# More filler matmuls in TensorE's planned idle time, in a recurrence and feed-forward kernel

## The chip, the core and the metric

The kernel runs on one NeuronCore of one Trainium2 chip, as one program. The metric is the device time of one execution in microseconds (us), lower is better. TensorE (PE in the profile) multiplies matrices into PSUM; a matmul appears there as a weight load (PEld) and a matmul. VectorE (DVE), ScalarE (ACT) and GpSimd (POOL) do the elementwise work, and SyncE (SP) issues transfers. Each engine runs its own instructions in the order in which they were emitted, and waits for others through semaphores. The profile also records which clock TensorE was granted, as a share of full speed.

## What is computed

Two parts stand in a row: a gated linear recurrence per head, and a mixing block with a feed-forward network. Inputs are float32: q, k, v, alpha of (4 batches, 8 heads, 768 steps, 48), and weights of 384 x 1536 and 1536 x 384.

```
# recurrence, per batch and head; state is 48 x 48
for t in range(768):
    state = alpha[t][:, None] * state + outer(k[t], v[t])
    y[t] = q[t] @ state
x = y, heads side by side                          # (4, 768, 384)
u = x + real(fft(fft(x, axis=1), axis=2))
un = (u - mean(u)) / sqrt(var(u) + 1e-6)           # over the 384 columns
out = u + relu(un @ w_ch1) @ w_ch2
```

## The kernel before

**Work.** Heads are handled in pairs, four pairs to a batch. For a pair, VectorE scans alpha into running products (`al`, `w`), TensorE transposes (`kt<-al`), forms products of keys and queries (`f<-w,al`), ScalarE copies them to `w`, GpSimd masks them, and TensorE multiplies them with values (`a<-vn,w`) and carries the state on (`a<-tt,w`). When a batch's four pairs are done, its y goes through the transforms as matmuls with constant matrices (`f<-cst,w`, then `a<-cst,x`), VectorE adds the results to y and normalises the rows (`qs<-y,mv,r`), TensorE transposes those (`f<-cst,qs`), and the feed-forward network follows: `f<-x,wt` makes 128 hidden rows, ScalarE and VectorE split them into two parts `h`, and `f<-wt,h` accumulates the output. Batch 0's attention and transform have no feed-forward work beside them; later batches' run beside the feed-forward network of the batch before.

**Order.** The functions of the kernel do not issue instructions. They record operations, and a planner (`Plan.emit`) then walks through them with a duration for each operation and a clock for each engine in planned microseconds, and writes one order for all engines. The order depends on the planner's durations, on keys that the code sets (`plan.key`) and on when buffers come free. The chip then runs that order with its own durations.

**Fillers.** When the planner puts an operation on TensorE at planned time t, later than its clock for TensorE, it writes small matmuls ahead of it, as many as fit when each is given `DUMMY` of planned time:

```
if op.engine == "PE" and self.idle and t < self.idle[2] and not self.open:
    for _ in range(int((t - max(clock["PE"], self.idle[1])) / DUMMY)):
        order.append(self.idle[0])
```

`self.idle[1]` is 1.0, `self.idle[2]` is `WARM`: no filler is planned at or after that time. `self.open` is true while the PSUM tile that fillers write to (`f2`, number 2) accumulates a feed-forward output. The fillers don't move the planner's clock, so no other operation is planned differently for them. A filler multiplies a tile of zeros by itself, 32 columns wide, into a corner of that tile that nothing reads (line 1144 of the profile, `f<-zero`):

```
plan.idle = (lambda: nc.tensor.matmul(warm[2][0:32, 480:512], zero.real(), zero.real(), start=True, stop=True), 1.0, WARM, ("f2", 2))
```

Being float32 with two passes, each leaves two records in the profile. On the chip a filler is an ordinary instruction in TensorE's row: what stands behind it starts after it. Where the tile was read by ScalarE just before, the first filler behind waits for that read. In the profile line 463 is the helper that records all other operations, and line 211 the one for relu on ScalarE.

Of the kernel before, what the change touches and what calls it, by code (L numbers as in the profile page):

```python
# [53 lines left out]
SPLIT = 388  # L54
KCK = -700.0
KF0 = -505.0
WARM = 120.0
DUMMY = 0.11
KTINY = 0.5 * 2.0**15 / (1.0 + 15.5 / 128.0)


# [113 lines left out]
class Plan:  # L175
# [176 lines left out]
    def emit(self):  # L352
# [35 lines left out]
        while placed < len(ops):  # L388
# [35 lines left out]
# [3 lines that stand above are left out]
# [54 lines left out]
def gla_mix_ffn(ctx: ExitStack, tc: tile.TileContext, alpha, kq, v, w1, w2, consts, rowtab, out):  # L481
# [660 lines left out]
    warm = plan.tags["f2"]["reals"]  # L1142
    if WARM:
        plan.idle = (lambda: nc.tensor.matmul(warm[2][0:32, 480:512], zero.real(), zero.real(), start=True, stop=True), 1.0, WARM, ("f2", 2))  # L1144
    with tc.manual_schedule():
# [147 lines left out]
```

## Time and profile before

| | |
|---|---|
| median of 3 runs | 567.91 us (567.4 to 568.93) |
| profiled execution | 566.41 us, its span 564.7 us |
| TensorE busy | 537.7 us, 95% of the span |
| VectorE, ScalarE, GpSimd busy | 406.4, 194.8, 57.5 us |
| mean granted TensorE clock | 0.94 |
| fillers | 924 records, 44.0 us of TensorE's busy time |

The span runs from the first to the last instruction; the execution's own time is 1.7 us longer. Times in the profile count from the span's start. A row in order of time gives start and length, the engine, the line, the operation with its output and inputs (buffer numbers left out), its shape, and in brackets how long the engine sat idle before it and who ended that. Matmuls overlap, so their spacing is shorter than the duration of one. TensorE's clock is 1.00 or 0.50 at any moment; a stretch's figure is a mean.

### The profile page before, as it was taken

The page shows a single profiled execution, that of the slowest core. Times are in us where ns is not written, and L with a number is a line of the kernel's source. Part 1 is how long each engine was busy: PE and PEld are TensorE (multiplying, and loading weights), DVE is VectorE, ACT ScalarE, POOL GpSimd, SP SyncE. Part 2 cuts the span into 40 slices and gives each one's busy share as a digit, 9 for nine tenths or more (in the row PEclk, how much of TensorE's full clock was granted, in tenths as well). Part 3 has the DMA queues.
Part 4 walks back from the last instruction along what each step waited for, and adds up shares of the span by engine and source line. Part 5 has one row for each costly group of instructions (what it writes and reads, how often), then busy time and mean ns, then how long its engine had stood idle before and what let it go on. Part 6 is the DMA issues. An engine that isn't in the chain of part 4 may idle for free.

```text
span 564.7 us, 10382 instructions
## 1 busy us (share of the span) xinstructions
PE 537.7 (95%) x4144; PEld 520.9 (92%) x4144; DVE 406.4 (72%) x1078; ACT 194.8 (34%) x428; POOL 57.5 (10%) x80
## 2 busy tenths in 40 slices
PE   7799989789999999969999999999999999999995
PEld 6689979678999999959999999999999999999995
DVE  7746996999599968799998859999977672312111
ACT  3262523343463433123555232354451221211110
POOL 0221230010100112000112110021222000000000
PEclk9657987898799999979999999999999999999998
DMA  8996480010320025010342510112003000101001
GB/s 217 258 375 151 165 281 22 2 46 29 100 67 0 2 76 165 28 43 1 96 125 79 168 43 0 50 43 71 21 2 126 2 0 2 43 0 37 7 0 46
DMA packets 16549, 42.22 MB, mean 75 GB/s; under 512 B 1904, under 2 KB 7088, under 8 KB 16496
## 3 DMA queue, kind: packets, MB, share of 16 engines
q1 hardware_dynamic: 15440, 39.08, 22.7%
q0 software_dynamic: 768, 2.36, 1.5%
q8 instruction: 34, 0.56, 0.4%
q14 instruction: 19, 0.16, 0.1%
q10 hardware_dynamic: 288, 0.07, 0.1%
HBM read 34.42 MB, written 7.08 MB: 73 GB/s over the span
## 4 chain that ended last, share of the span: by engine, by line
PE 86%; DVE 6%; DMA 3%; ACT 1%; issue 1%; SPq 1%; POOL 0%; ACTq 0%
PE f L463 58%; PE a L463 24%; PE f L1144 4%; DMA al<-in_alpha_dram 3%; DVE y L463 2%; DVE w L463 1%; DVE st L463 1%; SPq L463 1%; DVE x L463 1%; DVE al L463 0%; ACT c L463 0%; DVE h L463 0%; ACT wt L463 0%; ACT x L463 0%; ACT w L463 0%
## 5 line engine op out<-in xcount | busy, mean ns | idle before, releaser
L463 PE MATMUL f<-x,wt 128*128 128x384 f32 x864 | 180.5, 347 | 0.1
L463 PE MATMUL f<-wt,h 128*128 128x384 f32 x864 | 179.2, 343 | 0.1
L463 PEld LDWEIGHTS f<-x,wt 128*128 128x128 f32 x864 | 154.0, 192 | 0.9 <-ACT x L463 0.5
L463 PEld LDWEIGHTS f<-wt,h 128*128 128x128 f32 x864 | 151.3, 190 | 1.2 <-issue 0.5
L463 DVE SCALAR_TENSOR_TENSOR h<-f,h 128x384 fp32r<-128x384 f32 x96 | 53.2, 555 | 82.2 <-ACT h L211 80.9
L211 ACT ACTIVATE h<-f 128x384 fp32r<-128x384 f32 x96 | 47.1, 491 | 183.6 <-PE f L463 171.4
L463 POOL TENSOR_SCALAR_AFFINE_SELECT w<-w 128x512 f32<-128x512 f32 (+1 forms) x64 | 43.2, 696 | 340.4 <-ACT w L463 335.2
L463 PE MATMUL a<-vn,w 128*128 128x64 f32 x312 | 50.2, 290 | 0.0
L1144 PEld LDWEIGHTS f<-zero 128*32 128x32 f32 x924 | 39.3, 128 | 10.4 <-ACT w L463 4.1
L1144 PE MATMUL f<-zero 128*32 128x32 f32 x924 | 44.0, 213 | 5.1 <-ACT w L463 3.7
L463 PEld LDWEIGHTS a<-vn,w 128*128 128x128 f32 x312 | 47.5, 214 | 0.5
L463 PE MATMUL a<-cst,w 96*128 96x96 f32 (+10 forms) x267 | 34.5, 271 | 4.2 <-DVE r L463 4.2
L463 PEld LDWEIGHTS a<-cst,w 128*96 128x96 f32 (+7 forms) x267 | 32.9, 169 | 5.4 <-issue 4.5
L463 ACT COPY w<-a 128x512 f32<-128x512 f32 (+6 forms) x58 | 25.7, 482 | 34.0 <-PE a L463 31.6
L463 DVE TENSOR_TENSOR y<-y,a 128x191 f32<-128x191 f32 (+2 forms) x96 | 27.8, 344 | 12.0 <-PE a L463 12.0
L463 PE MATMUL a<-qs,qs 112*128 112x256 f32 x162 | 30.0, 290 | 0.0
L463 PE MATMUL a<-tt,w 112*128 112x96 f32 x134 | 29.6, 305 | 0.0
L463 DVE TENSOR_TENSOR sd<-y,y 128x288 f32<-128x288 f32 x32 | 13.3, 454 | 22.1 <-ACT y L463 22.1
L463 DVE TENSOR_TENSOR_SCAN w<-al,d 112x768 f32<-112x768 f32 (+1 forms) x17 | 28.8, 1694 | 0.1
L463 DVE TENSOR_TENSOR_SCAN al<-al,d 112x768 f32<-112x768 f32 (+1 forms) x17 | 28.2, 1657 | 0.0
L463 DVE TENSOR_TENSOR y<-y,f 128x384 f32<-128x384 f32 (+2 forms) x44 | 21.1, 514 | 7.9 <-PE f L463 7.6
L463 PEld LDWEIGHTS a<-qs,qs 112*128 112x128 f32 x162 | 24.9, 189 | 0.0
(123 smaller groups left out, 626.1 us busy)
## 6 DMA issues: line engine op xcount, KB each, us to landing
kq<-in_kq_dram SPq DMA_DIRECT2D x13, 672.0 KB, 5.9
wt<-in_w_dram SPq DMA_DIRECT2D x8, 768.0 KB, 10.4
al<-in_alpha_dram SPq DMA_DIRECT2D x15, 336.0 KB, 5.4
out_dram<-y SPq DMA_DIRECT2D x24, 192.0 KB, 1.9
vn<-in_v_dram SPq DMA_DIRECT2D x14, 296.0 KB, 2.9
wt<-in_w_dram SPq DMA_DIRECT2D x8, 384.0 KB, 9.1
scr<-y SPq DMA_DIRECT2D x4, 576.0 KB, 4.1
wt<-in_kq_dram SPq DMA_DIRECT2D x2, 672.0 KB, 14.4
```

The costliest lines, as they stand in the source:

```text
L211: return lambda out, x: e.activation(out, x, AF.Relu)
L463: op.ins = op.fns[op.engine](*[real(a) for a in op.args], **{k: real(x) for k, x in op.kwargs.items()})
L1144: plan.idle = (lambda: nc.tensor.matmul(warm[2][0:32, 480:512], zero.real(), zero.real(), start=True, stop=True), 1.0, WARM, ("f2", 2))
```

## The change

```
-WARM = 120.0
-DUMMY = 0.11
+WARM = 150.0
+DUMMY = 0.04
```

The planner fits one filler into each 0.04 of planned idle time instead of 0.11, and may do so up to planned time 150 instead of 120. In the order that comes out, TensorE has 1304 fillers in place of 462, in the same 39 places; the last place is the same. All other instructions of TensorE stand as before, and so do those of the four other engines.

TensorE at the start of the program, with the change marked (`f_2_55_120<-zero` are fillers, `cst,al` transposes of keys, `vn,kt` the state's products, `w,al` keys by queries):

```order
 L1289 UNCONDITIONAL_BRANCH
-L1144 MATMUL f_2_55_120<-zero 32x32 x52
+L1144 MATMUL f_2_55_120<-zero 32x32 x145
 L463 MATMUL a_48_113<-cst,al_40_105 128x112 x3
-L1144 MATMUL f_2_55_120<-zero 32x32 x7
+L1144 MATMUL f_2_55_120<-zero 32x32 x21
 L463 MATMUL f_0_53_118<-vn_46_111,kt_9_74 112x96 x3
-L1144 MATMUL f_2_55_120<-zero 32x32 x13
+L1144 MATMUL f_2_55_120<-zero 32x32 x36
 L463 MATMUL f_0_51_116<-w_1_2_67,al_40_105 128x128
```

Nothing moved; the three blocks of fillers grew.

TensorE before, between the last attention product of batch 0 (`tt,w`) and its first transform matmuls (`cst,w`):

```order
L463 MATMUL f_1_123_753<-tt_135,w_1_95_539 128x2x48
L1144 MATMUL f_2_110_666<-zero 32x32 x81
L463 MATMUL f_0_134_938<-cst,w_6_7_72 97x65
L1144 MATMUL f_2_110_666<-zero 32x32
L463 MATMUL f_1_135_942<-cst,w_6_7_72 96x65
L1144 MATMUL f_2_110_666<-zero 32x32
L463 MATMUL a_136_946<-cst,w_6_7_72 95x64
L1144 MATMUL f_2_110_666<-zero 32x32 x10
```

The same place now (the last numbers in the names count tiles and differ for that reason alone):

```order
L463 MATMUL f_1_123_1062<-tt_135,w_1_95_781 128x2x48
L1144 MATMUL f_2_110_975<-zero 32x32 x224
L463 MATMUL f_0_134_1444<-cst,w_6_7_72 97x65
L1144 MATMUL f_2_110_975<-zero 32x32 x3
L463 MATMUL f_1_135_1450<-cst,w_6_7_72 96x65
L1144 MATMUL f_2_110_975<-zero 32x32 x3
L463 MATMUL a_136_1456<-cst,w_6_7_72 95x64
L1144 MATMUL f_2_110_975<-zero 32x32 x27
```

The largest block grew from 81 to 224, and the small ones between transform matmuls from 1 to 3 and from 10 to 27.

TensorE now, from the last transform products of batch 0 (`cst,x`) to the transposes of its normalised rows (`cst,qs`):

```order
L463 MATMUL a_148_1799<-cst,x_141_1609 128x96
L463 MATMUL a_148_1799<-cst,x_141_1609 128x97
L1144 MATMUL f_2_137_1488<-zero 32x32 x169
L463 MATMUL f_0_149_2006<-cst,qs_10_75 128x128
L463 MATMUL f_0_150_2008<-cst,qs_10_75 128x128
L463 MATMUL f_1_151_2010<-cst,qs_10_75 128x128
L1144 MATMUL f_2_137_1488<-zero 32x32 x4
```

Before, the two blocks in it had 61 and 1; the rows around them are the same.

## The prediction

> **What bounds the kernel now.** I read the page first (which engine fills the span, and in which slices TensorE's clock is low), then the busy times stage by stage, then TensorE's rows in order of time, and last the rows of ScalarE and VectorE that release it. From the page: TensorE's share of the span, its clock in 40 slices of 14.1 us, and the group of the filler matmuls (line 1144).
>
> ```profile
> PE 537.7 (95%) x4144; PEld 520.9 (92%) x4144; DVE 406.4 (72%) x1078; ACT 194.8 (34%) x428; POOL 57.5 (10%) x80
> PEclk9657987898799999979999999999999999999998
> L1144 PE MATMUL f<-zero 128*32 128x32 f32 x924 | 44.0, 213 | 5.1 <-ACT w L463 3.7
> ```
>
> TensorE is the bound nearly everywhere, and what it is given to do counts. 462 fillers leave 924 records (two passes each), with 44.0 us of busy time already. The next table is busy time by stage (columns: stretch, length, then busy and count for PE, PEld, DVE, ACT, POOL; clock; DMA), and under it the fillers alone. I cut where TensorE waits or where the clock changes.
>
> ```profile
> 18.74:49.70 30.96, 30.96 (x259) 28.25 (x260) 18.85 (x46) 11.95 (x27) 6.33 (x6) 0.50 1.03 305
> 49.70:70.69 20.99, 20.91 (x242) 18.86 (x240) 15.91 (x38) 10.58 (x22) 4.34 (x8) 1.00 0.39 137
> 70.69:78.45 7.76, 5.32 (x163) 5.23 (x163) 7.22 (x21) 2.36 (x5) 1.14 (x1) 1.00 0.77 238
> 78.45:99.56 21.11, 20.68 (x254) 18.72 (x254) 16.18 (x51) 5.38 (x9) 3.61 (x3) 0.76 0.37 116
> 99.56:106.73 7.17, 4.06 (x124) 3.94 (x123) 7.17 (x33) 0.59 (x2) 0.00 (x0) 1.00 0.00 0
> 106.73:115.43 8.70, 8.68 (x92) 6.81 (x92) 7.90 (x22) 5.28 (x10) 0.00 (x0) 0.80 0.01 2
> 115.43:165.00 49.57, 46.73 (x284) 44.26 (x285) 41.80 (x91) 20.75 (x44) 4.88 (x8) 0.86 0.23 69
> 165.00:564.70 399.70, 388.85 (x2546) 384.49 (x2544) 276.66 (x730) 131.83 (x298) 35.22 (x49) 0.99 0.15 45
> ```
>
> ```profile
> 18.74:49.70 30.96, 10.02 (x155) 8.83 (x156) 0.50 1.03 305
> 49.70:70.69 20.99, 4.16 (x95) 3.38 (x93) 1.00 0.39 137
> 78.45:99.56 21.11, 8.91 (x178) 7.69 (x178) 0.76 0.37 116
> 106.73:115.43 8.70, 4.37 (x68) 3.57 (x68) 0.80 0.01 2
> ```
>
> Two facts decide the case. From 18.74 to 70.69 us TensorE is never idle for more than 0.08 us, and 14.2 us of that is fillers: what was planned as idle time is none on the chip, and fillers there already push real work back. And the clock is at half for 31 us (18.74 to 49.70), for 2 x (1 - 0.76) x 21.11 = 10.1 us of the transform stage and 2 x (1 - 0.80) x 8.70 = 3.5 us before the first feed-forward matmul.
>
> TensorE in order of time: start, length, what, and in brackets its idle time before.
>
> ```profile
> 1.04 5.21 PE L1144 MATMUL f<-zero 128*32 128x32 f32 x104 [1.04 <-DVE zero L463]
> 9.81 0.80 PE L463 MATMUL f<-vn,kt 128*112 128x96 f32 x6 [1.57 <-DMA vn<-in_v_dram]
> 11.48 0.71 PE L463 MATMUL f<-w,al 64*128 64x128 f32 x6
> 18.74 0.38 PE L1144 MATMUL f<-zero 128*32 128x32 f32 x6 [3.73 <-ACT w L463]
> 21.60 2.02 PE L1144 MATMUL f<-zero 128*32 128x32 f32 x34
> ...
> 24.52 1.01 PE L463 MATMUL a<-vn,w 128*128 128x64 f32 x4
> ...
> 58.31 0.58 PE L463 MATMUL a<-wt,w 128*128 128x64 f32 x4
> ...
> 70.69 5.32 PE L1144 MATMUL f<-zero 128*32 128x32 f32 x162
> 78.45 0.36 PE L463 MATMUL f<-cst,w 128*97 128x65 f32 x2 [2.44 <-ACT c L463]
> ...
> 106.73 0.55 PE L463 MATMUL f<-cst,qs 128*128 128x128 f32 x3 [3.11 <-DVE qs L463]
> ```
>
> **The price of a filler.** The block of 162 records takes 5.32 us; less the 0.17 us by which a block's last record outlasts the spacing, that is 32 ns a record at full clock, 64 ns a filler. At half clock 34 records in 2.02 us give 53 ns and 107 ns. The planner fits one filler into each 0.04 us of planned idle; at full clock it takes 0.064. So 1304 fillers last 83.5 us in at least 1304 x 0.04 = 52 us of planned idle, and every block outlasts its hole.
>
> A rule that speaks against this change, and by how much: the Trainium skill (TensorE: Matmul & The Clock Gate, "Wait — 56ns, not 53.3ns?") has successive matmuls start no closer than about 25 ns apart, however small. An estimate from that figure has a filler at 50 ns and the sum below at 22.3 - 2608 x 0.007 = 4 us instead of 22. The trace's 32 ns are taken.
>
> **The change part by part.** WARM from 120 to 150 costs and brings nothing: the fillers stand in the same 39 places, the last ahead of the same matmul, because from there the accumulator that they write to is open. No other instruction moves on any engine. So the change is DUMMY alone: 842 fillers more, all in front of real TensorE work. In each stage I take the fillers' new busy time (records x 0.032 + 0.17 a block) against the old, real work at half clock going to full clock if the gaps close (4 records of 64 columns take 1.01 us at 24.52 and 0.58 at 58.31, which with the last one's tail off is about half), and idle time that fillers absorb. That the clock stays full is my choice: it fell after the 3.73 us of idle ahead of 18.74, and with more fillers no gap of TensorE before 115 us stays above 1 us.
>
> Start to 18.74. The first block goes from 52 to 145: 186 records more x 0.032 = 6.0 us, the 0.9 us wait ahead of the first transpose absorbed, so +5.05 us. Then 14 fillers more (+0.9), the 1.57 us wait at 9.81 gone, 23 more (+1.5): TensorE reaches 11.48 about 5.8 us late. ScalarE copies what it makes then, which releases 18.74:
>
> ```profile
> 12.99 0.86 ACT L463 COPY w<-f 128x384 f32<-128x384 f32 x2
> 16.91 0.94 ACT L463 ACTIVATE c<-al,cm 112x768 uint8<-112x768 uint8 x1 [3.06 <-DMA al<-in_alpha_dram]
> 17.85 0.84 ACT L463 COPY w<-f 128x384 f32<-128x384 f32 x2
> ```
>
> The copies at 12.99 come at 18.8, the check of alpha no longer waits for its transfer and runs behind them, the copies at 17.85 end near 21.4 and TensorE goes on at 21.5: +2.75 us, the 3.73 us wait nearly used up.
>
> 18.74 to 70.69. Fillers 123 to 351 (16 blocks): 702 x 0.032 + 2.7 = 25.2 us against 14.2, +11.0. Real work at half clock 30.96 - 10.02 = 20.9, halved: -10.5. Together +0.5: the clock pays for the fillers and nothing is left. VectorE, ahead of TensorE there (18.85 of 30.96 us), doesn't get in the way.
>
> 70.69 to 78.45. One block, 81 to 224: 14.5 us in a hole of 7.76, +6.7. The 2.44 us wait goes, and the transform starts late.
>
> 78.45 to 99.56. 89 to 251 (10 blocks): 16.1 + 1.7 = 17.8 against 8.9, +8.9; real work at half clock is 10.1 less about 4.3 of fillers, halved: -2.9. Together +5.9.
>
> 99.56 to 106.73. 61 to 169: 11.0 us in 7.17, +3.8. What this block waits for is VectorE's chain from the last transform product to the normalised rows:
>
> ```profile
> 101.27 0.33 DVE L463 TENSOR_TENSOR y<-y,a 128x193 f32<-128x193 f32 x1
> ...
> 106.20 0.47 DVE L463 TENSOR_SCALAR qs<-y,mv,r 128x384 f32<-128x384 f32 x1
> 115.35 0.56 DVE L463 SCALAR_TENSOR_TENSOR h<-f,h 128x384 fp32r<-128x384 f32 x1 [0.80 <-ACT h L211]
> ```
>
> From 101.27 to 106.20 is 4.9 us: VectorE will have rows ready about 6 us before TensorE's 11 us of fillers end.
>
> 106.73 to 115.43. 34 to 100 (7 blocks): 7.6 against 4.4, +3.2, less about 0.5 of half clock: +2.7.
>
> Sum at the end of the last block: 2.75 + 0.5 + 6.7 + 5.9 + 3.8 + 2.7 = +22.3 us.
>
> Behind it TensorE is busy 46.73 of 49.57 us and then 388.85 of 399.70, so a delay is carried to the end but for what it had waited there: 2.84 us up to 165, as in
>
> ```profile
> 122.42 1.26 PE L463 MATMUL a<-w,al 64*128 64x128 f32 x12 [0.45 <-DVE x L463]
> 125.00 0.90 PE L463 MATMUL a<-cst,h 128*128 128x128 f32 x3 [1.32 <-ACT w L463]
> ```
>
> VectorE waits at 115.35 for the first feed-forward product, and so falls back nearly as far as TensorE; I allow it a lead of 0.8 us. Total +21.5 us on the profiled execution of 566.41, so 587.9; the median of the runs, 567.91, lies 1.5 above it: **589 us**, slower by 3.8%.
>
> **The rivals.** (1) The clock decides, and the result is faster: the added fillers only fill time in which TensorE waits, all of real work before 115 us runs at full clock, and 10.5 + 2.9 + 0.5 = 13.9 us come off: 554 us. For it: the clock did fall behind idle time (18.74). Against it: the busy 30.96 of 30.96. It decides if a filler record takes under 0.032 - 22.3 / 2608 = 0.0235 us. The Trainium skill (same page, "Why this matters for your kernels") asks for no TensorE gap of over about 3 us, which favours this rival; the trace agrees on the drop after 3.73 us. Chance 0.05.
>
> (2) The delay is partly given back: the wait of 2.84 us up to 165 goes, and so does the half clock there, 2 x (1 - 0.86) x 49.57 = 13.9 us at half, worth 6.9: 9.8 us less, 579 to 580. Against it: VectorE is delayed by the same matmuls. Chance 0.13.
>
> (3) The clock doesn't hold in the first attention stage: 20.9 us of real work stay at half clock, and the some 500 filler records there take 53 ns instead of 32, 10.5 + 10.6 us more, 610 us at most. Against it: at half clock a block of 48 fillers alone is 5 us of unbroken work, and the first block of all (104 records in 5.21 us, 50 ns each) already ends at the fast rate. A part of it, say 600 us, has 0.08.
>
> (4) No change, as the waits behind 70 us hide more and real work gains more than I have: 568, 0.02.
>
> My forecast has 0.72. The runs before spread over 0.3%, about what can be told from no change: faster 0.05, same 0.02, slower 0.93. The likeliest case's own range is 584 to 593: the start's phase of the clock (53 ns records for 1.3 us more or less), one stretch of 6.8 us at half clock more or less behind 115 us (3.4 us). With rival 2 below and part of rival 3 above, 579 to 597.
>
> **What would show it.** Filler records 2608, busy about 92 us (1304 x 0.064, 39 x 0.17, and 1.7 at the start while the clock is low). Full clock from 5 us to beyond 130. The transform's first matmul (78.45 before) at about 88 us, the transposes of the normalised rows (106.73) at about 126, the last block's end (115.43) at about 138, with no idle time of TensorE ahead of the first two. VectorE idle longer, waiting for TensorE. From 165 us on (187 after) all as before. Wrong if: records come at 25 ns or less; TensorE shows idle time ahead of those matmuls, so that the holes were longer than I read them; the clock falls inside the filler stages; or the stretch behind the last block is shorter by more than 4 us.

## The result, and the profile after

The changed kernel takes 607.27 us (median of 4 runs, 603.24 to 614.51) against 567.65 for the kernel before (4 runs, 562.95 to 568.93): a ratio of 1.069, 95% interval [1.060, 1.078]. Medians and ranges are of all runs, here and below; ratios leave out runs more than 1.5% above the fastest of their kernel. The prediction said 589, between 579 and 597: the sign was right, and the loss is nearly twice as large as forecast, 40.9 us between the two profiled spans instead of 21.5.

From the page of the changed kernel: the busy times, the clock in 40 slices of 15.1 us, the filler group, and the queue that brings instructions (packets, MB, share).

```profile
PE 582.4 (96%) x5828; PEld 566.0 (93%) x5828; DVE 406.3 (67%) x1078; ACT 195.0 (32%) x428; POOL 55.9 (9%) x80
PEclk9779998999977999999899999999999999999999
L1144 PE MATMUL f<-zero 128*32 128x32 f32 x2608 | 97.8, 202 | 8.1 <-issue 6.3
q8 instruction: 48, 0.79, 0.5%
```

The fillers are the 2608 records forecast, with 97.8 us instead of 92. New is the end of the third line: before, the idle time ahead of fillers was 5.1 us, most of it waits for ScalarE; now it is 8.1, and 6.3 of it is put down to "issue", which means that no semaphore and no transfer that the profile knows ended it. The last line had 34 packets on the page of the kernel before, and has 48 now.

TensorE of the changed kernel in order of time, read as the list in the prediction:

```profile
1.04 9.14 PE L1144 MATMUL f<-zero 128*32 128x32 f32 x223 [1.04 <-DVE zero L463]
12.52 3.67 PE L1144 MATMUL f<-zero 128*32 128x32 f32 x67 [2.34 <-issue]
...
21.41 2.59 PE L1144 MATMUL f<-zero 128*32 128x32 f32 x63 [2.18 <-issue]
...
30.59 1.06 PE L1144 MATMUL f<-zero 128*32 128x32 f32 x16
...
88.72 6.50 PE L1144 MATMUL f<-zero 128*32 128x32 f32 x196
95.65 0.30 PE L1144 MATMUL f<-zero 128*32 128x32 f32 x4 [0.43 <-issue]
...
97.92 9.15 PE L1144 MATMUL f<-zero 128*32 128x32 f32 x240 [0.45 <-issue]
106.99 0.38 PE L463 MATMUL f<-cst,w 128*97 128x65 f32 x2
...
134.23 10.89 PE L1144 MATMUL f<-zero 128*32 128x32 f32 x338
145.05 0.55 PE L463 MATMUL f<-cst,qs 128*128 128x128 f32 x3
...
156.71 0.95 PE L463 MATMUL f<-wt,h 128*128 128x384 f32 x4
```

The first block of fillers, 290 records of one instruction after another with nothing to wait for, breaks off after 223 and goes on 2.34 us later. The same happens at 19.2 and, in smaller pieces, from 95.2 to 98. Nothing of the kind is in the list of the kernel before.

Busy time by stage, cut at the gaps and where the stages of the prediction's table begin (the third row ends at 30.59, which was 18.74 before; 0 to 10.18 and 16.12 to 21.41 are left out; columns as there):

```profile
10.18:12.52 2.34, 0.00 (x1) 0.00 (x0) 1.06 (x3) 0.00 (x0) 0.00 (x0) 1.00 1.00 223
12.52:16.12 3.60, 3.60 (x68) 3.56 (x67) 0.00 (x0) 0.00 (x0) 0.00 (x0) 0.53 1.05 247
21.41:30.59 9.18, 9.18 (x110) 8.02 (x109) 2.53 (x7) 3.06 (x8) 1.52 (x3) 0.58 1.02 274
30.59:88.72 58.13, 55.98 (x955) 51.83 (x954) 34.92 (x83) 22.42 (x49) 11.47 (x13) 0.95 0.47 162
88.72:106.99 18.27, 16.46 (x449) 15.99 (x448) 17.73 (x50) 4.02 (x7) 3.04 (x3) 0.91 0.68 235
106.99:134.23 27.24, 26.81 (x582) 25.21 (x579) 7.49 (x27) 3.83 (x6) 0.00 (x0) 1.00 0.01 3
134.23:145.05 10.82, 10.82 (x340) 10.78 (x339) 9.63 (x37) 0.59 (x2) 0.00 (x0) 1.00 0.01 3
145.05:156.71 11.66, 11.51 (x227) 9.93 (x225) 4.87 (x10) 5.31 (x10) 0.00 (x0) 1.00 0.01 3
156.71:206.00 49.29, 46.64 (x283) 44.13 (x284) 40.63 (x90) 20.58 (x44) 4.89 (x8) 0.86 0.23 69
206.00:605.60 399.60, 389.12 (x2547) 384.69 (x2545) 276.93 (x730) 132.15 (x298) 34.80 (x49) 0.99 0.15 45
```

In the gap at 10.18 the DMA share is 1.00, and behind it the clock column falls to 0.53: the clock was lost just where fillers were meant to keep it. From 106.99 on, where the DMA engines are nearly idle, the same fillers run without a gap at full clock.

### The profile page after: what moved, and what is told of

Same layout as the page of the kernel before. It is cut to its first block, busy times and chain, and to the rows that moved or that the text cites. A ratio compares the mean times of both kernels' runs of the same rounds, so it can differ in the third digit from the quotient of the medians.

```text
span 605.6 us, 13750 instructions
## 1 busy us (share of the span) xinstructions
PE 582.4 (96%) x5828; PEld 566.0 (93%) x5828; DVE 406.3 (67%) x1078; ACT 195.0 (32%) x428; POOL 55.9 (9%) x80
## 4 chain that ended last, share of the span: by engine, by line
PE 91%; DVE 4%; issue 2%; POOL 1%; ACT 1%; ACTq 0%
PE f L463 54%; PE a L463 21%; PE f L1144 16%; POOL w L463 1%; DVE w L463 1%; DVE y L463 1%; DVE x L463 0%; DVE al L463 0%; DVE h L463 0%; ACT wt L463 0%; ACT x L463 0%; DVE tt L463 0%; DVE wt L463 0%; DVE st L463 0%; ACT b L463 0%
## 5 line engine op out<-in xcount | busy, mean ns | idle before, releaser
L1144 PE MATMUL f<-zero 128*32 128x32 f32 x2608 | 97.8, 202 | 8.1 <-issue 6.3
L1144 PEld LDWEIGHTS f<-zero 128*32 128x32 f32 x2608 | 92.8, 118 | 13.0 <-issue 8.3
L463 PE MATMUL a<-vn,w 128*128 128x64 f32 x312 | 47.4, 278 | 1.7 <-POOL w L463 1.7
L463 PEld LDWEIGHTS a<-vn,w 128*128 128x128 f32 x312 | 44.5, 201 | 2.4 <-POOL w L463 2.0
L463 PE MATMUL a<-tt,w 112*128 112x96 f32 x134 | 27.9, 290 | 0.0
L463 ACT COPY y<-a 128x288 f32<-128x288 f32 x27 | 10.8, 400 | 47.0 <-PE a L463 47.0
## 6 DMA issues: line engine op xcount, KB each, us to landing
wt<-in_w_dram SPq DMA_DIRECT2D x8, 768.0 KB, 12.6
```

Of the source, the lines that this page charges most:

```text
L463: op.ins = op.fns[op.engine](*[real(a) for a in op.args], **{k: real(x) for k, x in op.kwargs.items()})
```

## The experiments

The line of the filler matmul is 1144 in the kernels of the case, and up to nine lines further down in some experiments. Where a kernel ran only once, its single time is given.

**Same filler time, fewer instructions (e_wide).** Against the changed kernel, a filler is 96 columns wide:

```
-DUMMY = 0.04
+DUMMY = 0.10
-    zero = fixed([P, 32], "zero")
+    zero = fixed([P, 96], "zero")
-  ...nc.tensor.matmul(warm[2][0:32, 480:512], zero.real(), zero.real(), ...
+  ...nc.tensor.matmul(warm[2][0:32, 416:512], zero.real()[:, 0:32], zero.real(), ...
```

> The changed kernel with fillers three times as wide (96 columns instead of 32) and one for each 0.10 of planned idle time: 510 fillers in the same 39 places, about as much filler time (510 x 0.16 us = 82 us against 1304 x 0.064 = 83), with two fifths of the instructions. Theory 'fetch': TensorE's instructions come to it by DMA, 16 KB at a time, and where transfers fill the DMA engines long blocks of small fillers run out of instructions; idle time that the profile puts down to issue (6.3 us ahead of fillers in the changed kernel) and the half clock behind it are the part that the prediction lacked. Then issue idle falls under 1 us, the start (up to the first fillers behind ScalarE's copies) ends near 21 us instead of 30, and the time is near the predicted 588 us (583 to 595). Rival 'pace': the stalls belong to the time that the fillers fill, however many instructions it takes: 603 to 610 us and the same stalls.

Measured: 596.15 us (594.42 to 597.05) against 571.32, ratio 1.046 [1.036, 1.055]: 1 us above the range of "fetch", 7 below that of "pace". TensorE of this kernel in order of time:

```profile
1.10 11.11 PE L1144 MATMUL f<-zero 128*32 128x96 f32 x116 [1.10 <-DVE zero L463]
...
21.32 0.68 PE L1144 MATMUL f<-zero 128*32 128x96 f32 x6 [0.21 <-ACT w L463]
...
75.14 14.87 PE L1144 MATMUL f<-zero 128*32 128x96 f32 x178
89.94 0.38 PE L463 MATMUL f<-cst,w 128*97 128x65 f32 x2
...
117.48 11.24 PE L1144 MATMUL f<-zero 128*32 128x96 f32 x134
128.65 0.55 PE L463 MATMUL f<-cst,qs 128*128 128x128 f32 x3
```

No block is broken, though each of the two long ones lasts as long as the prediction gave the changed kernel's (14.87 and 11.24 us against 14.5 and 11.0). The wait at 18.74 ends at 21.32, the transform begins at 89.94, the rows are transposed from 128.65: 2.6, 11.5 and 21.9 us later than before, where the prediction's running sum has 2.75, 10.0 and 19.6. So the late instructions of the changed kernel come from the number of fillers, not from the time that they fill. Between the two profiled spans, 605.6 and 592.7, lie 12.9 us: the gaps and the half clock made 16.4 by the first output matmul behind the fillers (156.71 against 140.27), and this kernel loses 3.5 more behind it.

**The first three blocks as before (e_first_old).** `/ DUMMY` becomes `/ (0.11 if t < 12.0 else DUMMY)`: 52, 7 and 13 fillers there, all others as changed.

> The changed kernel with the first three filler blocks as before the change (52, 7 and 13 in place of 145, 21 and 36), all others as changed. 'Fetch': the 4.5 us of issue idle up to 21.4 us go with the long blocks, the start ends near 18.8 us as before, the clock falls to half at about 19 us and is back within about 10 us; the time falls by the 11.9 us of the start and by up to 6 us of half clock, less what the fall at 19 us costs: 588 to 597 us. Rival 'count': only the 130 fillers taken out count, 130 x 0.064 = 8.3 us less what idle time hid of them (2.5): 601 us.

Measured: 600.58 us (590.7 to 603.39). Three runs, the profiled one among them, lie at 599.84 to 603.39, where "count" had 601, and one at 590.7, within the range of "fetch": the times do not decide. The rows do. The start was mended: TensorE went on at 18.68. But the breaks turned up elsewhere:

```profile
49.88 2.56 PE L1144 MATMUL f<-zero 128*32 128x32 f32 x76 [1.29 <-issue]
...
84.09 4.21 PE L1144 MATMUL f<-zero 128*32 128x32 f32 x128 [0.38 <-issue]
90.56 4.77 PE L1144 MATMUL f<-zero 128*32 128x32 f32 x103 [2.26 <-issue]
```

Between the last two breaks stand 128 records. The queue's packets say why that is the number: 14 packets and 0.23 MB more for 842 fillers of two passes, each a weight load and a matmul, 3368 instructions; that is 241 instructions for one packet of 16 KB, or 256 if the added part is not a whole number of packets, and 256 instructions are 128 records. The places of the breaks say the same. Counted in the traces (TensorE's matmuls, weight loads and its few others), those of over half a microsecond inside filler blocks stand behind instruction 449 and 705 in the changed kernel, 1473 and 3009 here, 3265 and 3521 in e_load and 4801 in e_load3 below: 449 and whole multiples of 256 more, in every run. At 32 ns a packet of small fillers lasts 4.1 us; at the 84 ns of a wide one (178 in 14.87) 10.7. The Trainium skill (Runtime: NRT & Kernel Launch, "Instruction fetch mechanics") says that an engine's instructions come in blocks of 16 KiB, 256 at a time, over a DMA queue of their own while the current ones run, and calls the cost of a crossing mostly hidden. The count agrees; "hidden" holds here for wide fillers, and not for small ones while data is read from DRAM.

**The first three blocks alone (e_first_only).** The kernel before with `/ (0.04 if t < 12.0 else 0.11)`.

> The kernel before with the first three filler blocks alone as changed (145, 21, 36), all others as before. 'Fetch': the start ends 10 to 13 us later than before with two stalls of about 2 us put down to issue; 577 to 582 us. Rival 'count': 2.75 us, as the prediction had it for the start: 570 to 572 us.

Measured: 567.64 us (559.57 to 578.41), ratio 0.988 [0.973, 1.002]: missed by both theories. The start did break off, 3.70 and 1.94 us, and ended 9.2 us late. But then the following attention stage, which had taken 51.95 us (18.74 to 70.69) with a clock of 0.50 in its first 31, took 39.31 from 27.90 on:

```profile
27.90:67.21 39.31, 38.88 (x497) 35.07 (x497) 35.52 (x85) 22.57 (x49) 7.11 (x14) 1.00 0.79 260
```

The clock is full, and VectorE is busy 35.52 of 39.31. Coming late, TensorE found its inputs ready and waited 0.43 us in all. So the half clock before was worth up to 12.6 us in this stage, and a late start can buy it back. The four runs of this kernel lie far apart, and the clock goes with them, 0.966 in the fastest and 0.938 in the slowest; which stretch lost it in the runs without a trace is not shown.

**No fillers (e_none).** `WARM = 0.0`.

> No fillers at all. If fillers earn their time by the clock (they hold it up, or bring it back up), TensorE's clock is at half through most of the first 115 us, real work of some 17 us between 50 and 71 us doubles, and the time is above that before: 575 to 590 us. If the fillers before the change already cost more than they earn, the time is below 565: their 14.2 us between 18.74 and 70.69 stand in a stretch where TensorE never idles, and 555 us is possible.

Measured: 563.34 us (562.65 to 566.12), ratio 0.987 [0.978, 0.996]: at most a small gain over the kernel before, and no loss. The last line is the changed kernel's, of the same matmuls as the one above it.

```profile
31.74 2.18 PE L463 MATMUL a<-vn,kt 128*112 128x96 f32 x10 [5.02 <-ACT kt L463]
...
83.25 0.88 PE L463 MATMUL f<-cst,w 128*97 128x65 f32 x4 [7.69 <-issue]
...
89.03 3.73 PE L463 MATMUL f<-cst,w 128*97 128x128 f32 x16 [0.68 <-DVE w L463]
...
108.44 2.18 PE L463 MATMUL f<-cst,qs 128*128 128x128 f32 x9 [9.78 <-DVE qs L463]
```

```profile
118.14 2.00 PE L463 MATMUL f<-cst,w 128*97 128x128 f32 x16
```

Without fillers TensorE waits here 5.02, 7.69 and 9.78 us, and the last of these marks is 1.7 us later than before (106.73). And it works at half clock up to 93 us: the 16 transform matmuls take 3.73 us, in the changed kernel 2.00. (The clock column reads 1.00 there and is wrong: this trace has no entry for the clock before 93.5 us.) The fillers of the kernel before hold the clock for a time, but the time that they take from real work is about as large. Where the gain lies is not shown: the profiled execution, the slowest of the four, has a span of 564.4 us, the kernel before 564.7. The 7.69 us put down to issue are the hole that took 5.32 us of fillers and a wait of 2.44 us for ScalarE before; outside a block of like instructions that word says nothing about late instructions. The Trainium skill (TensorE: Matmul & The Clock Gate, "Why this matters for your kernels") asks for no gap over about 3 us. With three longer ones the clock was low here, as it says, and they still cost no more than filling them.

**Holding the clock at its first loss (e_hold).** The kernel before with 18 wide fillers more in the 3.73 us wait ahead of 18.74.

> The kernel before with one block added: 18 fillers of 96 columns (about 2.9 us) ahead of the first product of masked scores with values, in the 3.7 us in which TensorE waits for ScalarE at 15 to 18.7 us; all else as before. If that wait is what takes the clock down at 18.98 us, the clock stays full there, the 20.9 us of real work at half clock and 10 us of fillers up to 49.7 us halve (VectorE's 18.9 us of work and transfers hold back part of it), and the time falls by 8 to 14 us, to 555 to 562 on the scale of 569. If the clock falls anyway: no change within 2 us.

Measured: 569.88 us (561.92 to 573.61), ratio 0.997 [0.991, 1.003]: missed. The wait was filled, and the clock was full from 14 to 31 us (it had been at half for 3.4 us before, behind a wait of 2.15 us for a transfer). Then TensorE, no longer slow, ran into the next thing that was not there, keys (ScalarE's copy of them stands behind the check of alpha, which waits for its transfer), and the clock was lost 12 us later than before:

```profile
31.53 2.18 PE L469 MATMUL a<-vn,kt 128*112 128x96 f32 x10 [4.32 <-ACT kt L469]
```

**A table of fillers (e_placed).** 228 wide fillers, counted by hand for the kernel's own waits (27, 12, 5, 20 at the start, 44 ahead of the transform, 14 and 41 in it and behind it).

> Fillers by hand: 96 columns wide, about 230 of them, in the same 39 places, long where TensorE truly waits on the chip (start, behind the first scores, ahead of the transform, ahead of the normalised rows' transposes: 27, 12, 20, 44, 41) and few or none elsewhere. If short instruction streams don't stall and filled waits hold the clock, TensorE's clock is full to 115 us, stage 18.74 to 70.69 takes 36 to 40 us instead of 52, and the last filler block ends near 98 to 102 us instead of 115: 550 to 557 us. If fillers cost wherever they stand, or the clock falls between them: 562 to 570, as without fillers.

Measured: 563.94 us (556.95 to 571.77), ratio 0.987 [0.982, 0.993]. The transform began at 75.26 instead of 78.45 and the rows were transposed at 99.09 instead of 106.73, but another 3.39 us wait for keys at 29.63 and a stretch of half clock from 130 to 154 us took part of it back: the expectation's second case. Its ratio is that of the kernel without fillers, and none of the other kernels has one clearly below.

**What delays the instructions (e_load, e_load_wide, e_load2, e_load2_wide, e_load3, e_load3_wide).** Six kernels that ran once each: the changed kernel, or e_wide, with transfers added that nothing waits for, to fill the DMA engines where they were idle. The first pair stores 16 x 590 KB, issued by ScalarE once batch 0's attention is done, the second 16 x 393 KB from the finished part of the transform (the edit of the second pair, less its line for the planner):

```
+if m == 1 and scr is scratch[0] and plan.direct is None:
+    for x in extra_out:
+        A.dma_start(x.rearrange("(a p) n -> p a n", p=P), yt[:, 0:2])
+        ...
```

> The changed kernel with extra transfers: 16 copies of a 590 KB tile to memory that nothing reads, issued by ScalarE once batch 0's attention is done, so that the DMA engines are full between about 92 and 125 us, where TensorE works through long filler blocks (107 to 134 us) that ran without a stall before. 'Fetch': idle time put down to issue appears ahead of fillers there, 2 us or more, and long blocks run slower than 32 ns a record. Rival 'start': stalls belong to the start of the program, none in that stretch (under 0.5 us).

> The same extra transfers in the kernel with 96-column fillers (510 instead of 1304, the same filler time). 'Fetch': with two fifths of the instructions TensorE doesn't run dry: issue idle under 0.5 us in that stretch. If the extra transfers stall TensorE in another way (operands, ScalarE late), the stalls are as in the kernel with small fillers.

Measured: 625.36 and 606.6 us. In the first the stores went out from 87 to 122 us, ahead of the quiet stretch that they were meant for, and ScalarE's issuing held up its cast of weights, for which VectorE waited 23.94 us with the transform's inputs behind it in its row (TensorE's waits ahead of `cst,w` are 12.68 and 16.21 us). What can be read is the block of fillers in front of it: whole with wide fillers, broken with small ones, by 2.44 and 0.60 us where the changed kernel had four gaps of 0.43 to 0.48.

```profile
94.86 5.60 PE L1151 MATMUL f<-zero 128*32 128x32 f32 x128 [2.44 <-issue]
```

> The changed kernel with extra transfers put where it had none: 16 copies of 393 KB from the finished part of batch 0's transform to memory that nothing reads, issued by ScalarE when that part is done. They fill the DMA engines from about 127 to 145 us, the stretch of the two blocks of 212 and 338 filler records, which ran at 32 ns a record without a gap. No other instruction of TensorE or VectorE moves, and nothing on TensorE depends on these transfers. 'Fetch': TensorE runs dry inside those blocks, 2 us or more of idle time put down to issue, as in the first 22 us. Rival 'start' (stalls belong to the start of the program or to something else there): no gap, the blocks as before.

> The same extra transfers at the same place in the kernel with 96-column fillers (84 and 134 records there). 'Fetch': with two fifths of the instructions no gap, under 0.5 us of issue idle. If the transfers slow TensorE in another way, as by its reads of operands: gaps or slower records here too.

Measured: 621.45 and 600.75 us. Now the load lay on the block of 338 records, at a DMA share of 1.03, and the block did not break:

```profile
135.00:140.00 5.00, 5.00 (x164) 5.00 (x161) 0.00 (x0) 0.00 (x0) 0.00 (x0) 1.00 1.03 360
```

The transfers from 133 to 140 us of this run:

```profile
q10 hardware_dynamic: 1716, 2.49, 101.3%
q8 instruction: 2, 0.03, 1.7%
```

The expectation missed: full DMA engines alone do not make the instructions late. The two packets of instructions that came under the stores took 0.017 x 16 x 7 / 2 = 0.95 us each. The time was lost to waits of 10.41 and 9.69 us for VectorE's rows, which stood behind ScalarE's issuing. These stores read on-chip memory in rows of 1.5 KB; the transfers of the start and of 95 us, under which blocks broke, read from DRAM. The last pair therefore copies 8 x 672 KB from DRAM to DRAM in long rows:

```
+if m == 0 and scr is scratch[0] and plan.direct is None:
+    ...
+    for i, x in enumerate(extra_out):
+        A.dma_start(x, kq[i])
+        ...
```

> This is the changed kernel with eight copies of 672 KB from DRAM to DRAM, with long rows, issued by ScalarE once batch 0's transform copies are done (about 122 us), which nothing waits for; it adds transfers and changes no computation. Theory A, TensorE's instructions come late when the DMA engines are reading other data from DRAM: the block of 338 small matmuls, which ran unbroken for 10.89 us in the changed kernel, or the 212 ahead of it, shows at least one gap of 1 us or more put down to issue at a DMA share near 1. Theory B, the late instructions of the first 100 us have to do with something else (branching, the start of the program): the two blocks run unbroken in spite of the copies. By both the time is longer than the changed kernel's 607 us by what the issuing of the copies and the waits for shared DMA engines cost, 5 to 20 us.

Measured: 622.03 us against 568.74 before, as both theories had it; the gap decides for A.

```profile
126.22 5.70 PE L1153 MATMUL f<-zero 128*32 128x32 f32 x174
136.64 2.19 PE L1153 MATMUL f<-zero 128*32 128x32 f32 x38 [4.72 <-issue]
...
140.71 11.78 PE L1153 MATMUL f<-zero 128*32 128x32 f32 x338
```

The block of 212, whole in the changed kernel, breaks for 4.72 us in the middle of the copies, and the one of 338, which runs when they are done, does not. The transfers of two stretches of this run, the gap and the later block, show the instruction queue's packets and their share of 16 engines:

```profile
q8 instruction: 1, 0.02, 2.1%
...
q8 instruction: 2, 0.03, 1.1%
```

One packet comes in the 4.72 us of the gap and takes 0.021 x 16 x 4.72 = 1.6 us on its engine; in the 11.71 us of the later block two take 0.011 x 16 x 11.71 = 2.1, 1.0 each. None came in the 5.70 us of fillers ahead of the gap. In the changed kernel a packet starts 1.8 us into this block (128.10, the block from 126.34), with no data moving, and takes 1.36 us; here it starts 7.5 us into it (133.69), 1.8 us into the gap, and TensorE goes on 1.3 us after its end. So the packet itself was little slower, and most of the delay was in front of it.

> The eight copies from DRAM to DRAM of the run before this, with 96-column fillers in place of 32-column ones: the same filler time with two fifths of the instructions, so that one arrival of instructions lasts 2.5 times as long. Theory A, late arrivals: the 4.72 us gap inside the filler block at about 132 us is gone or under 1.5 us, the clock stays full there, and the time is that of the kernel with 96-column fillers, 596 us, and 0 to 10 us for the copies. Rival, the copies hold TensorE up in another way (they slow whatever runs, or its access to memory): a gap of 3 us or more at the same place, and 608 us or more.

Measured: 587.09 us against 569.88 before. The same copies, with wide fillers, on the stretch from 110 to 122.4 us: the copies' queue fills the engines, an instruction packet comes among them, and no break is seen.

```profile
q10 hardware_dynamic: 186, 4.00, 103.1%
q8 instruction: 1, 0.02, 0.6%
```

```profile
109.48 7.12 PE L1153 MATMUL f<-zero 128*32 128x96 f32 x84
...
117.59 11.24 PE L1153 MATMUL f<-zero 128*32 128x96 f32 x134
128.77 0.55 PE L465 MATMUL f<-cst,qs 128*128 128x128 f32 x3
```

The gap is gone, as theory A had it, and the time is below what both had. The marks are those of e_wide (117.59 and 128.77 against 117.48 and 128.65); what makes the run 7.4 us shorter than e_wide (585.3 against 592.7 us of span) comes later, and is told below. The two kernels ran on different chips.

## Why the prediction was right in sign and too small

**Right: the price and the last three terms.** A small filler costs 64 ns and outlasts its 0.04 of planned time. The running lateness of the changed kernel at its marks (18.74 to 30.59, 70.69 to 88.72, 78.45 to 106.99, 99.56 to 134.23, 106.73 to 145.05, the next matmul from 115.56 to 156.71, the span's end from 564.7 to 605.6) gives each stage's share:

| term | predicted | measured |
|---|---|---|
| start to 18.74 | +2.75 | +11.85 |
| 18.74 to 70.69 | +0.5 | +6.2 |
| 70.69 to 78.45 | +6.7 | +10.5 |
| 78.45 to 99.56 | +5.9 | +6.1 |
| 99.56 to 106.73 | +3.8 | +3.65 |
| 106.73 to 115.43 | +2.7 | +2.8 |
| behind it | -0.8 | -0.2 |

Nearly nothing was given back, and the clock behind the last block is 0.86 as it was, so rival 2 falls for this kernel.

**Wrong: "that the clock stays full is my choice".** The working took for granted that TensorE always has its next instruction, and that more fillers leave no gap above 1 us. The three wrong terms are short by 9.1, 5.7 and 3.8 us. From the rows of after: in the start, gaps of 2.34 and 2.18, and half clock for 2 x 0.47 x 3.60 + 2 x 0.42 x 9.18 = 11.1 us, worth 5.5: together 10.1. In the attention stage, 2 x 0.05 x 58.13 = 5.8 us at half clock, worth 2.9, and 2.15 us of idle time, most of it waits for GpSimd: 5.0. In the large block, 18.27 - 16.46 = 1.8 of gaps and 3.3 us at half clock, worth 1.6: 3.5. The sum is 18.6 of the missing 18.6, closer than its parts, which miss by 1.0, 0.7 and 0.3 and cancel: that is luck. Each prices half clock as half of its time, an estimate. That the gaps and the half clock behind them are due to the number of instructions is shown by e_wide, and by the breaks that stand whole multiples of 256 instructions apart; that copies such as those of e_load3 make instructions late, and stores such as those of e_load2 do not, by one run of each.

**The rivals.** Rival 1, the clock decides, fell with the price: records came at 32 ns. Rival 3, the clock does not hold, has the nearest times (600 us for a part, 610 at most), but by luck: the stage that it names ran at 0.95, and the clock was lost at another place and for another reason, because the fillers starve themselves in the start. The list of what would show the forecast wrong named both signs, idle time ahead of those matmuls and a clock that falls inside the filler stages.

**The sum without gaps.** The marks forecast at about 88, 126 and 138 us came at 106.99, 145.05 and 156.71; in e_wide, which is what the working described, fillers of that time without gaps at full clock, they came at 89.94, 128.65 and 140.27, the last 24.7 us late where the sum had 22.3. Its span is 28.0 longer than before, e_load3_wide's, with its mark at 140.38, only 20.6. Between them lies the clock behind the fillers: the windows from 160 to 180 us of e_wide and of e_load3_wide.

```profile
160.00:180.00 20.00, 18.43 (x102) 17.05 (x100) 10.04 (x28) 6.13 (x14) 2.20 (x4) 0.66 0.23 68
```

```profile
160.00:180.00 20.00, 18.43 (x141) 16.89 (x140) 16.40 (x42) 11.03 (x22) 2.09 (x4) 1.00 0.40 117
```

At 0.66 it is half clock for 2 x 0.34 x 20 = 13.6 us, up to 6.8 us of the 7.4. Where the clock falls once the fillers are over was in no term of the sum, and moves two runs with equal marks that far apart; rival 2's give-back by the clock came in e_load3_wide and not in the changed kernel.

**Left open.** Why the four short gaps from 95.2 to 98 come about 8 instructions apart; they stand 34 to 11 instructions ahead of 3265, a place of the series where e_load breaks. Which property of the added copies makes the difference, their source in DRAM or their long rows: both changed between e_load2 and e_load3. Length alone hardly fits the start, where 7.33 MB moved in 2940 packets, 2.5 KB each (0 to 31 us), against 1.5 KB under e_load2's stores. And whether the half clock or the gaps cost more in the changed kernel, since one brings the other.

## What to carry to other kernels

A filler has two prices, its spacing in the engine's row (here 64 ns, in a hole planned at 40) and its share of the instruction stream; before adding many tiny ones, count records per packet (128 here, 4.1 us) and look whether DRAM reads fill the DMA engines at that time, and if fillers are needed at all, take few long ones. First run the kernel without any: here it was no slower than with the tuned number (ratio 0.987 [0.978, 0.996]), and in e_hold a clock held at one wait only brought TensorE sooner to the next. In a profile, idle time put down to "issue" inside an unbroken block of like instructions is the sign of an engine that waits for its own program; whether the breaks stand 256 instructions apart tells.

## What the runs showed of the hardware that was not expected

TensorE stood still for 2.34, 2.18 and up to 4.72 us with nothing to wait for, its instructions arriving in packets of 16 KB, while copies read DRAM; under stores from on-chip memory at the same DMA share of 1.03 it did not. Behind a gap of 2.34 us the clock went to half at 12.5 us and stayed there for 3.4 us, a gap shorter than the 3.73 us that cost the clock before. Without fillers TensorE ran at half clock up to 93 us, and the kernel was no slower. And a start that ends 9.2 us late (e_first_only) cost nothing, since the following stage at full clock was 12.6 us shorter.
